# Six additions of output weights, moved from VectorE to a copy and an accumulating DMA

## The chip, the core and the metric

The kernel runs on one core of a Trainium2 chip. The metric is the device time in microseconds of one execution. The engines are named as the profile names them: PE is TensorE (matmuls), DVE is VectorE, ACT is ScalarE, POOL is GpSimd, and SP is the engine that issues most DMAs. Each engine works through its own instructions in order; a wait for a semaphore holds what stands behind it.

## The reference

Three steps follow each other on 4608 rows (tokens) of 512 columns: attention in chunks of 64, a gated layer with a norm, and a layer with a rational function.

```python
x = attention(q, k, v)                        # 8 x 8 heads, 576 rows, chunks of 64
xn = x / rms(x) * rms_g
g, val = xn @ w_gate, xn @ w_val              # 512 -> 1536
x = (g * sigmoid(g) * val) @ w_out            # 1536 -> 512
h = x @ w_in                                  # 512 -> 2048
P = a[0] + a[1] * h + a[2] * h**2 + a[3] * h**3
Q = 1 + abs(b[0]) * abs(h) + abs(b[1]) * h**2
out = (P / (Q + 1e-06)) @ w_out2              # 2048 -> 512
```

All is float32. The factors of `q` and `k` only set the spread of the inputs.

## The kernel before

Each float32 operand of a matmul is held as two words, a high one (rounded by ACT) and a low one (the rest, from a subtraction on DVE), and a product is three matmuls: high by high, high by low, low by high. The 4608 rows are nine blocks of 512. Many products are done with seven block products in place of eight, on sums and differences of quarters of both operands.

The work is a long list of turns. `at_turn` (L470) puts a step on a turn, `spread` (L638) puts the steps of a generator on successive turns, and `do` (L473) runs what a turn holds. Tables of turn numbers at the head of the file set where side work goes.

The change lies where the gate products end and the products with `w_out` begin, some 640 us into the program. `items` (L810) lists the latter: six items of block 0, called item 0 to item 5 below (24 matmuls each, plain, into the banks `a0_0` to `a0_3`), then items of 12 matmuls for pairs of blocks: B11 and B21 on plain weights, T2, T1, T3 and B22 on sums of weights (`so`), N4 on plain ones. Item 0 is on turn 252, the first item with `so` (T2) on turn 264.

For each item `high` (L882) casts the high word on ACT and `low` (L886) subtracts for the low word on DVE (L891), three items ahead, into `rring`, which has four places; a place is free once PE has done with its item. `uring` holds what `fetch` loads from `ud`.

`left_sums` (L830) makes the sums of weights for `f` = 0, 2, 4. It adds the two words of a weight back together (L835, two additions of 128x1024 into the pair `xo`), forms four sums of quarters (L839, 128x512 each), and splits them into `so` (L846 on ACT, L848 on DVE). `xo` takes buffers of the tag "t", of which there are three; `stage_left` has them for its raw weights (`raw2`) before. `LEFT_SUMS_AT` (L46) is the table of its turns, four steps to a turn.

In this stage only ACT keeps the order in which the code is written:

```python
        with tc.manual_schedule(engines={mybir.EngineType.Activation}):
```

DVE, PE, SP and POOL are ordered by the scheduler of the library, from its own estimates, when the program is built. The last instructions of the stage before are those of `finish` (L549): L511 and L558 work on the last gate products (`sa`), and L558 frees their PSUM banks, which `a0_1` takes next.

Of the kernel before, what the change touches and what calls it, by code (L numbers as in the profile page):

```python
# [9 lines left out]
F32 = mybir.dt.float32  # L10
# [4 lines left out]
ALU = mybir.AluOpType  # L15
# [7 lines left out]
U = 4  # L23
# [19 lines left out]
OPEN_AT = 237  # L43
START_AT = (244, 252)
QUAD_AT = (277, 271, 270, 274, 288, 285, 289, 288, 299, 304, 294, 307, 305, 320, 324, 324)
LEFT_SUMS_AT = (255, 254, 264)  # L46
EARLY = 3
BLOCK0 = (
    (-20, "fetch", 0), (-18, "ring", 0), (-17, "split", 0, "B11"), (-16, "split", 0, "B21"), (-15, "sum", 0, "T1"),
    (-14, "split", 0, "T1"), (-14, "sum", 0, "T3"), (-12, "ring", 1), (-11, "split", 0, "B22"), (-10, "sum", 0, "T2"),  # L50
# [6 lines left out]
def fused_kernel(  # L57
# [11 lines left out]
    nc = tc.nc  # L69
# [74 lines left out]
    buffers = {}  # L144
# [28 lines left out]
    def stage(f):  # L173
        words = raw_tile(2 * f + 1)
        yield
        hi, lo = (s2([P, W], f"{n}q_{f}", F32R) for n in ("hi", "lo"))
        yield from words_to_pair(*words, lambda: (hi, lo))
        for n, x in enumerate((hi, lo)):
            nc.sync.dma_start(out=wqd[f // U][:, n, f % U], in_=x.bitcast(F32))
        yield  # L180
# [3 lines left out]
    def stage_left(g):  # L184
        one, two = (raw_tile(4 * g + 2 * n) for n in range(2))
        yield
        yield from words_to_whole(*one)
        yield from words_to_whole(*two)
        x, y = (w[0].bitcast(F32) for w in (one, two))

        def put(at, x, name):
            hi, lo = (s2([P, W], f"{n}{name}_{g}", F32R)[:, :x.shape[1]] for n in ("hi", "lo"))
            yield from split(x, hi, lo)
            for n, z in enumerate((hi, lo)):
                nc.sync.dma_start(
                    out=wld[g][:, at:at + x.shape[1] // (2 * P), n, :],
                    in_=z.bitcast(F32).rearrange("p (k c) -> p k c", c=2 * P),
                )
            yield

        yield from put(0, x, "a")
        yield from put(6, y[:, W // 2:], "d")
        a11, a12, a21, a22 = (z[:, k * W // 2:(k + 1) * W // 2] for z in (x, y) for k in range(2))
        for o, i, j, op in ((a22, a21, a22, ALU.add), (a21, a11, a21, ALU.subtract), (a11, a22, a11, ALU.subtract), (a12, a12, a11, ALU.subtract)):
            nc.vector.tensor_tensor(out=o, in0=i, in1=j, op=op)
            yield
        yield from put(2, x, "s")
        yield from put(4, y, "u")
# [261 lines left out]
    def at_turn(turn, what, *of):  # L470
        plan.setdefault(turn, []).append((what, of))
# [166 lines left out]
    def spread(turn, steps, gap=1, each=1, most=60):  # L638
        for n in range(most):
            for _ in range(each):  # L640
                at_turn(turn + n * gap, next, steps, None)
# [54 lines left out]
    with ExitStack() as phase:  # L696
# [13 lines left out]
        def two_halves(source, u, keys):  # L710
            one, other = (unit(source, u, keys, p) for p in halves)
            next(one)
            next(other)
            yield
            yield from one
            yield from other
# [57 lines left out]
        for g in range(NF2 // 2):  # L774
            steps = stage_left(g)
            at_turn(STAGE_AT[g], next, steps)
            spread(STAGE_FROM[g], steps, 1, STAGE_EACH[g], 24 // STAGE_EACH[g])
        for u in range(3):
            steps = two_halves("wo", u, outs[u])
# [23 lines left out]
        with tc.manual_schedule(engines={mybir.EngineType.Activation}):  # L803
            KH = NF1 // 2
# [25 lines left out]
            def left_sums(f):  # L830
                xs = [sb.tile([P, 2, W], F32, tag="t", bufs=3, name=f"xo{f}_{n}") for n in range(2)]
                for n, x in enumerate(xs):
                    u, k = divmod(f + KH * n, U)
                    w = buffers["wo", u][1][:, :, k:k + 2].bitcast(F32)
                    nc.vector.tensor_tensor(out=x, in0=w[:, 0], in1=w[:, 1], op=ALU.add)  # L835
                    yield
                (a11, a21), (a12, a22) = ((x[:, :, :W // 2], x[:, :, W // 2:]) for x in xs)
                for o, x, y, op in ((a22, a21, a22, ALU.add), (a21, a11, a21, ALU.subtract), (a11, a22, a11, ALU.subtract), (a12, a12, a11, ALU.subtract)):
                    nc.vector.tensor_tensor(out=o, in0=x, in1=y, op=op)  # L839
                    yield  # L840
                for n, x in enumerate(xs):
                    u, k = divmod(f + KH * n, U)
                    w = sums_o[u][:, :, k:k + 2]
                    for m in range(2):
                        wt["so", f + KH * n + m] = w[:, :, m]
                    nc.scalar.copy(w[:, 0], x)  # L846
                    yield
                    nc.vector.tensor_tensor(out=w[:, 1], in0=x, in1=w[:, 0].bitcast(F32), op=ALU.subtract)  # L848
                    yield
# [8 lines left out]
            for n in range(NF2):  # L858
                steps = stage(n)
                at_turn(QUAD_AT[n], next, steps)  # L860
                spread(QUAD_AT[n] + 3, steps, 1, 2, 5)
            for f in range(0, KH, 2):
                spread(LEFT_SUMS_AT[f // 2], left_sums(f), 1, 4, 3)

            def sums_of(i):
                if i >= len(items) or items[i][0] is None:
# [89 lines left out]
            for t in range(NSB):  # L956
                running = {}
                used = 0
                for q, k in ORDER:
# [5 lines left out]
                    while True:  # L965
                        u = used // 8 + 2
# [24 lines left out]

            for turn, what, *of in BLOCK0:
                at_turn(end_o + turn, {"fetch": fetch_x2, "ring": x2_ring, "split": x2_split, "sum": x2_sum, "lefts": load_lefts,
                                       "work": make_work, "gg": make_gg, "quad": make_quad}[what], *of)

            def prepare(i):
                do(TURN[0])
                high(i + LEAD)
                sums_of(i + LEAD + 1)
                low(i + LEAD)  # L1000
# [47 lines left out]
            whole_acc, banks = [], []  # L1048
            for i in range(len(items) - 2 * EARLY):
                prepare(i)  # L1050
# [4 lines left out]
    def last_items():  # L1055
        for i in range(len(items) - 2 * EARLY, len(items)):
            prepare(i)
            todo = list(item_products(i))
            for n, of in enumerate(todo):
                nc.tensor.matmul(**of)  # L1060
                if n + 1 == len(todo):
                    item_end(i)
                yield

    with tc.manual_schedule(engines={mybir.EngineType.Activation, mybir.EngineType.DVE, mybir.EngineType.PE}):
# [76 lines left out]
        for p in range(NPAIR + 3):  # L1142
# [28 lines left out]
            if c is not None:  # L1171
                Tc = T_of.pop(c).rearrange("p e w -> p (e w)")
                r = ring["gg"][:, c % 2]
                for e in range(2):
# [3 lines left out]
                        out=r[:, 1, es], in0=Tc[:, es], in1=r[:, 0, es].bitcast(F32), op=ALU.subtract  # L1178
# [97 lines left out]
```

## Time and profile before

| what | us |
|---|---|
| median of 3 runs | 1670.3 |
| the three runs | 1670.16 to 1670.75 |
| the profiled execution | 1669.83 |
| its span, first to last instruction | 1668.0 |
| PE busy | 1656.3 |
| DVE busy | 1436.5 |
| ACT busy | 1055.7 |
| POOL busy | 331.0 |

The span is the time between the first and the last instruction of the profiled execution; 1.83 us of that execution lie around it. PE is busy 99% of the span. The granted TensorE clock is a share of full speed, 2.4 GHz.

### The profile page before, as it was taken

How to read it: one execution, taken by the hardware profiler on the slowest of the kernel's cores; microseconds unless marked ns; L12 is line 12 of the kernel's file. 1: busy time of each engine (PE TensorE's matmuls, PEld its weight loads, DVE VectorE, ACT ScalarE, POOL GpSimd, SP SyncE). 2: the span in 40 equal slices, each digit the busy share in tenths (PEclk: the TensorE clock that was granted, in tenths of full speed). 3: DMA queues.
4: the chain of work that ended last, by engine and by line, in shares of the span. 5: the costliest groups of instructions: out<-in, count | busy, mean ns of one | idle time of the engine just before them, and what ended most of it. 6: DMA issues, size and time to landing. Idle time of an engine off the chain costs nothing.

```text
span 1668.0 us, 28366 instructions
## 1 busy us (share of the span) xinstructions
PE 1656.3 (99%) x10956; PEld 1424.0 (85%) x10956; DVE 1436.5 (86%) x1762; ACT 1055.7 (63%) x1592; POOL 331.0 (20%) x286
## 2 busy tenths in 40 slices
PE   9999999999999999999999999999999999999999
PEld 7788888888888887888888899898999999989897
DVE  7978878877788788898997899999999999999986
ACT  7734445555465563566566777777777777777775
POOL 1000000000000000000012334343343434343321
PEclk9999999999999999999999999999999999999999
DMA  9547997878988998468757865655555555555551
GB/s 336 216 161 241 338 316 268 321 254 322 339 293 308 378 340 291 151 228 284 249 170 290 325 209 195 202 202 201 198 195 198 195 199 197 202 198 202 177 196 63
DMA packets 138694, 402.41 MB, mean 241 GB/s; under 512 B 13504, under 2 KB 58560, under 8 KB 124736
## 3 DMA queue, kind: packets, MB, share of 16 engines
q1 hardware_dynamic: 138416, 400.35, 67.9%
q8 instruction: 86, 1.41, 0.3%
q10 hardware_dynamic: 144, 0.26, 0.1%
q14 instruction: 48, 0.39, 0.1%
HBM read 308.29 MB, written 92.27 MB: 240 GB/s over the span
## 4 chain that ended last, share of the span: by engine, by line
PE 96%; DVE 1%; ACT 1%; DMA 1%; issue 1%; POOL 0%; DVEq 0%
PE o L1100 24%; PE h L1081 22%; PE sa L538 11%; PE sb L538 9%; PE ob L1052 6%; PE oa L1052 6%; PE v L501 5%; PE g L501 5%; PE xs L290 2%; PE a L1052 2%; PE tp L357 1%; PE tp L360 1%; PE ob L1060 0%; PE oa L1060 0%; DMA raw<-in_w_dram 0%
## 5 line engine op out<-in xcount | busy, mean ns | idle before, releaser
L1100 PE MATMUL o<-w,ggring 128*128 128x512 f32 x1728 | 418.6, 391 | 0.0
L1081 PEld LDWEIGHTS h<-x2ring,lefts 128*128 128x128 f32 x2982 | 377.3, 191 | 13.9 <-PE h L1081 2.1
L1081 PE MATMUL h<-x2ring,lefts 128*128 128x256 f32 x2982 | 382.7, 283 | 1.0 <-ACT both L1188 0.2
L1100 PEld LDWEIGHTS o<-w,ggring 128*128 128x128 f32 x1728 | 315.2, 188 | 60.6 <-POOL ggring L1177 0.5
L1177 POOL TENSOR_TENSOR ggring<-T,ggring 128x512 fp32r<-128x512 f32 x142 | 181.6, 1299 | 406.1 <-ACT ggring L1176 406.1
L671 POOL TENSOR_TENSOR x2ring<-x2r,x2ring 128x512 fp32r<-128x512 f32 x63 | 116.6, 1857 | 450.4 <-PE oa L1052 356.9
L1156 ACT ACTIVATE work<-h 128x1024 f32<-128x1024 f32 x72 | 73.9, 1026 | 164.7 <-PE h L1081 163.7
L884 ACT CAST rring<-uring 128x1024 fp32r<-128x1024 f32 x90 | 94.0, 1051 | 76.4 <-PE oa L1052 24.5
L1193 DVE SCALAR_TENSOR_TENSOR work<-work 128x1024 f32<-128x1024 f32 x72 | 133.9, 1860 | 2.5
L891 DVE TENSOR_TENSOR rring<-uring,rring 128x1024 fp32r<-128x1024 f32 x90 | 112.2, 1255 | 18.4 <-ACT rring L884 18.2
L1158 DVE SCALAR_TENSOR_TENSOR work<-work,small 128x1024 f32<-128x1024 f32 x72 | 92.1, 1280 | 27.8 <-ACT work L1157 27.8
L538 PE MATMUL sa<-right,left 128*128 128x512 f32 x432 | 111.2, 394 | 0.0
L501 PE MATMUL g<-xT,w 128*128 128x512 f32 (+1 forms) x444 | 109.9, 391 | 1.3 <-ACT w L135 0.6
L538 PE MATMUL sb<-right,left 128*128 128x512 f32 x432 | 108.8, 392 | 0.0
L501 PE MATMUL v<-xT,w 128*128 128x512 f32 (+1 forms) x444 | 106.5, 387 | 0.0
L1194 DVE SCALAR_TENSOR_TENSOR T<-T,small,work 128x1024 f32<-128x1024 f32 x72 | 99.9, 1387 | 2.5
L339 POOL TENSOR_SCALAR ssq<-ssq 128x1 f32<-128x1 f32 x36 | 7.3, 204 | 452.1 <-ACT xf L337 438.0
L501 PEld LDWEIGHTS g<-xT,w 128*128 128x128 f32 x444 | 80.1, 188 | 18.1 <-DVE w L137 0.9
L538 PEld LDWEIGHTS sb<-right,left 128*128 128x128 f32 x432 | 80.3, 188 | 16.9 <-DVE u L511 0.3
L501 PEld LDWEIGHTS v<-xT,w 128*128 128x128 f32 x444 | 80.8, 188 | 16.2
L1161 DVE SCALAR_TENSOR_TENSOR T<-T,small,h 128x1024 f32<-128x1024 f32 x72 | 92.2, 1281 | 2.5
L538 PEld LDWEIGHTS sa<-right,left 128*128 128x128 f32 x432 | 79.9, 188 | 16.2
(190 smaller groups left out, 2972.5 us busy)
## 6 DMA issues: line engine op xcount, KB each, us to landing
lefts<-wld SPq DMA_DIRECT2D x71, 1536.0 KB, 6.5
left<-wsd SPq DMA_DIRECT2D x30, 2048.0 KB, 9.8
ud<-u SPq DMA_DIRECT2D x108, 256.0 KB, 3.4
uring<-ud SPq DMA_DIRECT2D x54, 512.0 KB, 5.8
raw<-in_w_dram SPq DMA_DIRECT2D x36, 512.0 KB, 6.2
lefts<-wld SPq DMA_DIRECT2D x71, 256.0 KB, 2.8
wsd<-cb SPq DMA_DIRECT2D x48, 256.0 KB, 3.6
raw<-in_w_dram SPq DMA_DIRECT2D x10, 1024.0 KB, 9.8
```

Of the source, the lines that this page charges most:

```text
L501: nc.tensor.matmul(out=acc[:, ts], lhsT=w[:, wh, wk], rhs=x[:, kk, xh, ts], start=kk == 0 and n == 0, stop=kk == KD - 1 and n == 2,)
L538: nc.tensor.matmul(out=acc, lhsT=lhs[:, wh, kk * P:(kk + 1) * P], rhs=rhs[:, kk, xh, :], start=start and kk == 0 and m == 0, stop=kk == 1 ...
L671: nc.gpsimd.tensor_tensor(out=lo, in0=x, in1=hi.bitcast(F32), op=ALU.subtract)
L884: nc.scalar.copy(slot(i)[0], u_of(*items[i]))
L891: nc.vector.tensor_tensor(out=lo, in0=u_of(t, n, f), in1=hi.bitcast(F32), op=ALU.subtract)
L1052: nc.tensor.matmul(**of)
L1081: nc.tensor.matmul(out=out_, lhsT=lhs[:, wh, kk * P:(kk + 1) * P], rhs=rhs[:, kk, xh, :], start=start and kk == 0 and m == 0, stop=kk == 1 ...
L1100: nc.tensor.matmul(out=acc2[j][m], lhsT=ring["gg"][:, p % 2, rh, e * W + m * P:e * W + (m + 1) * P], rhs=ring["quad", f // U][:, wh, f % U ...
L1161: nc.vector.scalar_tensor_tensor(out=T, in0=T, scalar=a1, in1=H, op0=ALU.add, op1=ALU.mult)
L1177: (nc.vector if c == NPAIR - 1 else nc.gpsimd).tensor_tensor(out=r[:, 1, es], in0=Tc[:, es], in1=r[:, 0, es].bitcast(F32), op=ALU.subtract)
L1193: nc.vector.scalar_tensor_tensor(out=V, in0=V, scalar=-2.0, in1=R, op0=ALU.add, op1=ALU.mult)
L1194: nc.vector.scalar_tensor_tensor(out=T, in0=T, scalar=a0, in1=V, op0=ALU.add, op1=ALU.mult)
```

## The change

In `left_sums` the two additions L835 are replaced by DMAs, in two steps: SP copies the high word of both weights into `xo`, and POOL then issues two DMAs that add the low word to what lies in `xo`. The first step is put on a turn of its own, `SUM_AHEAD` = 2 turns ahead of the rest. The table of turns changes from (255, 254, 264) to (256, 262, 253), so that `f` = 4 now comes first, then `f` = 0, then `f` = 2. In the changed program the lines behind L835 stand further down: L839 is L845, L846 is L852, L848 is L854, L891 is L899.

```diff
--- before.py
+++ after.py
@@ -43,8 +43,9 @@
 OPEN_AT = 237
 START_AT = (244, 252)
 QUAD_AT = (277, 271, 270, 274, 288, 285, 289, 288, 299, 304, 294, 307, 305, 320, 324, 324)
-LEFT_SUMS_AT = (255, 254, 264)
+LEFT_SUMS_AT = (256, 262, 253)
 EARLY = 3
+SUM_AHEAD = 2
 BLOCK0 = (
     (-20, "fetch", 0), (-18, "ring", 0), (-17, "split", 0, "B11"), (-16, "split", 0, "B21"), (-15, "sum", 0, "T1"),
     (-14, "split", 0, "T1"), (-14, "sum", 0, "T3"), (-12, "ring", 1), (-11, "split", 0, "B22"), (-10, "sum", 0, "T2"),
@@ -832,8 +833,13 @@
                 for n, x in enumerate(xs):
                     u, k = divmod(f + KH * n, U)
                     w = buffers["wo", u][1][:, :, k:k + 2].bitcast(F32)
-                    nc.vector.tensor_tensor(out=x, in0=w[:, 0], in1=w[:, 1], op=ALU.add)
-                    yield
+                    nc.sync.dma_start(out=x, in_=w[:, 0])
+                yield
+                for n, x in enumerate(xs):
+                    u, k = divmod(f + KH * n, U)
+                    w = buffers["wo", u][1][:, :, k:k + 2].bitcast(F32)
+                    nc.gpsimd.dma_start(out=x, in_=w[:, 1], accum_op=ALU.add)
+                yield
                 (a11, a21), (a12, a22) = ((x[:, :, :W // 2], x[:, :, W // 2:]) for x in xs)
                 for o, x, y, op in ((a22, a21, a22, ALU.add), (a21, a11, a21, ALU.subtract), (a11, a22, a11, ALU.subtract), (a12, a12, a11, ALU.subtract)):
                     nc.vector.tensor_tensor(out=o, in0=x, in1=y, op=op)
@@ -860,7 +866,9 @@
                 at_turn(QUAD_AT[n], next, steps)
                 spread(QUAD_AT[n] + 3, steps, 1, 2, 5)
             for f in range(0, KH, 2):
-                spread(LEFT_SUMS_AT[f // 2], left_sums(f), 1, 4, 3)
+                steps = left_sums(f)
+                at_turn(LEFT_SUMS_AT[f // 2] - SUM_AHEAD, next, steps)
+                spread(LEFT_SUMS_AT[f // 2], steps, 1, 4, 3)
 
             def sums_of(i):
                 if i >= len(items) or items[i][0] is None:
```

The one-line label that came with the change names something else (the last output tile's products in runs of 256 columns, each half stored by itself). The diff has nothing of that; this text goes by the diff.

How the instructions move, at three places. A name such as `xo4_1` is buffer 1 of the pair for `f` = 4. DMAHW and DMASW are the semaphores of DMAs that were issued by SP and by POOL.

On DVE, at the end of the gate products and the start of block 0, before:

```order
L558 TENSOR_TENSOR u7_9_6727<-u7_9_6727,sa2_9_6741 128x512 [waits PE_49]
L511 SCALAR_TENSOR_TENSOR u7_11_6951<-u7_11_6951,sa2_10_6767 128x512 [waits DMAHW7_49,Activation_49]
L835 TENSOR_TENSOR xo2_1_7045<-w2_6709 128x1024
L558 TENSOR_TENSOR u7_11_6951<-u7_11_6951,sa2_11_6789 128x512 [waits DVE_49,PE_49]
L839 TENSOR_TENSOR xo2_1_7045<-xo2_0_7044,xo2_1_7045 128x2x256 [waits DVE_49]
L835 TENSOR_TENSOR xo0_0_7078<-w0_6352 128x1024
L891 TENSOR_TENSOR rring1_6738<-uring1_6736,rring1_6738 128x2x512 [waits DMAHW1_49,Activation_49]
L891 TENSOR_TENSOR rring0_6737<-uring1_6736,rring0_6737 128x2x512 [waits DMAHW3_49,Activation_49]
L891 TENSOR_TENSOR rring1_6738<-uring1_6736,rring1_6738 128x2x512 [waits DMAHW2_49,Activation_49]
L839 TENSOR_TENSOR xo2_0_7044<-xo2_0_7044 128x2x256 [waits DVE_49]
L839 TENSOR_TENSOR xo2_0_7044<-xo2_1_7045,xo2_0_7044 128x2x256 [waits DVE_49]
L839 TENSOR_TENSOR xo2_1_7045<-xo2_1_7045,xo2_0_7044 128x2x256 [waits DVE_49]
```

and now:

```order
L559 TENSOR_TENSOR u7_9_6727<-u7_9_6727,sa2_9_6741 128x512 [waits PE_49]
L512 SCALAR_TENSOR_TENSOR u7_11_6951<-u7_11_6951,sa2_10_6767 128x512 [waits DMAHW7_49,Activation_49]
L559 TENSOR_TENSOR u7_11_6951<-u7_11_6951,sa2_11_6789 128x512 [waits DVE_49,PE_49]
L845 TENSOR_TENSOR xo4_1_6955<-xo4_0_6954,xo4_1_6955 128x2x256 [waits DMASW1_49,DMASW0_49]
L845 TENSOR_TENSOR xo4_0_6954<-xo4_0_6954 128x2x256 [waits DVE_49]
L845 TENSOR_TENSOR xo4_0_6954<-xo4_1_6955,xo4_0_6954 128x2x256 [waits DVE_49]
L845 TENSOR_TENSOR xo4_1_6955<-xo4_1_6955,xo4_0_6954 128x2x256 [waits DVE_49]
L899 TENSOR_TENSOR rring1_6738<-uring1_6736,rring1_6738 128x2x512 [waits DMAHW2_49,Activation_49]
L899 TENSOR_TENSOR rring0_6737<-uring1_6736,rring0_6737 128x2x512 [waits DMAHW3_49,Activation_49]
L899 TENSOR_TENSOR rring1_6738<-uring1_6736,rring1_6738 128x2x512 [waits DMAHW7_49,Activation_49]
L899 TENSOR_TENSOR rring0_6737<-uring1_6736,rring0_6737 128x2x512 [waits DMAHW0_49,Activation_49]
```

Before, L835 stood ahead of the last L558 and between the others; the low words of items 2, 1 and 3 (the three L891) came ahead of the last three L839. Now the last L558 follows L511 directly, and the four L845 of `f` = 4, which wait for both accumulating DMAs, stand ahead of all the low words (L899: items 2, 1, 3 and 4).

On SP, some 15 us ahead of that place, before:

```order
L824 DMA uring1_6736<-ud_0_74 128x1024 [waits DMAHW1_49]
L824 DMA uring1_6736<-ud_0_74 128x1024 [waits DMAHW2_49]
L828 DMA uring0_6735<-ud_2_76 128x1024 [waits DMAHW3_49,DVE_49]
L514 DMA ud_8_82<-u8_8_6652 128x512 [waits DMAHW4_49,DVE_49]
L195 DMA wld_7_94<-his_7_6888 128x2x256 [waits DMAHW5_49,Activation_49]
L195 DMA wld_7_94<-los_7_6889 128x2x256 [waits DMAHW6_49,DVE_49]
L514 DMA ud_8_82<-u8_10_6885 128x512 [waits DMAHW7_49,DVE_49]
L824 DMA uring1_6736<-ud_0_74 128x1024 [waits DMAHW0_49]
```

and now:

```order
L836 DMA xo4_0_6954<-w1_6514 128x1024 [waits DMAHW1_49]
L825 DMA uring1_6736<-ud_0_74 128x1024 [waits DMAHW2_49]
L829 DMA uring0_6735<-ud_2_76 128x1024 [waits DMAHW3_49,DVE_49]
L515 DMA ud_8_82<-u8_8_6652 128x512 [waits DMAHW4_49,DVE_49]
L196 DMA wld_7_94<-his_7_6888 128x2x256 [waits DMAHW5_49,Activation_49]
L196 DMA wld_7_94<-los_7_6889 128x2x256 [waits DMAHW6_49,DVE_49]
L515 DMA ud_8_82<-u8_10_6885 128x512 [waits DMAHW7_49,DVE_49]
L836 DMA xo4_1_6955<-w2_6709 128x1024 [waits DMAHW0_49]
```

The copies into `xo4_0` and `xo4_1` stand in places that loads into `uring1` had (items 3 and 4 of block 0); these loads now come after the last store to `ud`.

On PE, in item 1 of block 0, before:

```order
L1052 MATMUL a0_0_6989<-rring0_6737,w0_6352 128x512 [waits Activation_49]
L1052 MATMUL a0_0_6989<-rring0_6737,w0_6352 128x512 [waits DVE_49]
L1052 MATMUL a0_0_6989<-rring0_6737,w0_6352 128x512
L1052 MATMUL a0_1_6990<-rring0_6737,w0_6352 128x512 x3
```

and now:

```order
L1060 MATMUL a0_0_6993<-rring0_6737,w0_6352 128x512 [waits Activation_49]
L1060 MATMUL a0_1_6994<-rring0_6737,w0_6352 128x512
L1060 MATMUL a0_2_6995<-rring0_6737,w0_6352 128x512
L1060 MATMUL a0_3_6996<-rring0_6737,w0_6352 128x512
L1060 MATMUL a0_0_6993<-rring0_6737,w0_6352 128x512 [waits DVE_49]
L1060 MATMUL a0_0_6993<-rring0_6737,w0_6352 128x512
```

The scheduler has pulled the products of item 1 that need only the high word, one for each bank, ahead of the first that waits for DVE's low word.

## Rows read from the trace of the kernel before

**Rows 1.** The page, part 1: busy us (share of the span) and instructions.

```profile
PE 1656.3 (99%) x10956; PEld 1424.0 (85%) x10956; DVE 1436.5 (86%) x1762; ACT 1055.7 (63%) x1592; POOL 331.0 (20%) x286
```

**Rows 2.** Busy time by stretch, 620 to 700 us; the columns stand first.

```profile
core 0: us, PE busy (x) PEld busy (x) DVE busy (x) ACT busy (x) POOL busy (x), PEclk, DMA share, GB/s
...
620.00:640.00 20.00, 20.00 (x89) 16.30 (x87) 16.90 (x29) 10.20 (x17) 0.00 (x0) 1.00 0.96 304
640.00:660.00 20.00, 18.72 (x83) 15.47 (x83) 16.46 (x19) 6.81 (x8) 0.00 (x0) 1.00 0.98 368
660.00:680.00 20.00, 20.00 (x90) 16.56 (x89) 20.00 (x20) 8.08 (x9) 0.00 (x0) 1.00 0.24 79
680.00:700.00 20.00, 20.00 (x90) 16.55 (x89) 19.67 (x21) 11.51 (x14) 0.00 (x0) 1.00 0.30 93
```

**Rows 3.** Waits of PE, 580 to 720 us: total us, times, longest.

```profile
PE a L1052 <- DVE u L558: 1.3, 1, 1.3
```

**Rows 4.** Timeline of DVE: start us, us, instruction, count [idle before <-what ended it].

```profile
628.55 0.69 DVE L570 TENSOR_TENSOR c<-c,sb 128x512 f32<-128x512 f32 x1 [2.90 <-PE sb L538]
...
638.89 0.68 DVE L511 SCALAR_TENSOR_TENSOR u<-u,sa 128x512 f32<-128x512 f32 x1
639.49 1.21 DVE L835 TENSOR_TENSOR xo<-w 128x1024 f32<-128x1024 f32 x1
640.62 0.68 DVE L558 TENSOR_TENSOR u<-u,sa 128x512 f32<-128x512 f32 x1
...
642.96 3.48 DVE L891 TENSOR_TENSOR rring<-uring,rring 128x1024 fp32r<-128x1024 f32 x3
646.37 0.68 DVE L839 TENSOR_TENSOR xo<-xo 128x512 f32<-128x512 f32 x1
647.08 1.42 DVE L839 TENSOR_TENSOR xo<-xo,xo 128x512 f32<-128x512 f32 x2
```

**Rows 5.** Timeline of PE, the same columns.

```profile
639.23 0.84 PE L1052 MATMUL a<-rring,w 128*128 128x512 f32 x3
641.36 32.25 PE L1052 MATMUL a<-rring,w 128*128 128x512 f32 x141 [1.28 <-DVE u L558]
673.45 8.32 PE L1052 MATMUL oa<-rring,w 128*128 128x512 f32 x36
681.61 8.32 PE L1052 MATMUL ob<-rring,w 128*128 128x512 f32 x36
689.77 8.32 PE L1052 MATMUL oa<-rring,so 128*128 128x512 f32 x36
```

**Rows 6.** Timeline of SP, 634 to 635 us.

```profile
634.58 0.51 SPq L824 DMA_DIRECT2D uring<-ud  x1
```

**Rows 7.** DMA issues of 634.5 to 635.0: count, KB each, median us to landing.

```profile
uring<-ud SPq DMA_DIRECT2D x1, 512.0 KB, 5.8
```

**Rows 8.** All loads into uring from 600 to 720 us.

```profile
DMA to landing us min/median/max: 3.6/5.9/10.4
```

**Rows 9.** DMA issues of 642.1 to 642.6 us.

```profile
uring<-ud SPq DMA_DIRECT2D x2, 512.0 KB, 6.4
```

**Rows 10.** Busy time by stretch at the end (columns of rows 2).

```profile
1664.00:1666.00 2.00, 0.25 (x2) 0.00 (x0) 0.00 (x0) 0.60 (x1) 0.00 (x0) 1.00 0.47 181
1666.00:1668.00 2.00, 0.00 (x0) 0.00 (x0) 0.00 (x0) 0.00 (x0) 0.00 (x0) 0.78 0.21 81
```

**Rows 11.** Busy time of POOL alone: us, busy (count), clock, DMA share, GB/s.

```profile
560.00:820.00 260.00, 0.00 (x0) 1.00 0.75 261
```

**Rows 12.** The page, part 6: DMA issues of the whole program.

```profile
raw<-in_w_dram SPq DMA_DIRECT2D x10, 1024.0 KB, 9.8
```

**Rows 13.** DMA issues of 590 to 710 us.

```profile
raw<-in_wo_dram SPq DMA_DIRECT2D x2, 1024.0 KB, 14.7
```

## The prediction

> **What bounds the kernel now.** I read the page first: PE is busy 1656.3 us of a span of 1668.0, DVE 1436.5 [rows 1]. Nothing else comes near, so time can only be won where PE waits, and lost where PE is made to wait. A gain of all PE's idle time would be 11.7 us, start and end of the program included. Then the stretches around the changed lines: from 620 to 700 us PE is busy in full but for 1.28 us in 640 to 660, while DVE is busy 16.46 to 20.00 us of each 20, and the DMA engines are nearly full (0.96, 0.98) until 660 and nearly idle behind it [rows 2]. Then PE's own waits from 580 to 720: there is one, 1.3 us, and it ends with DVE's L558 [rows 3]. The two timelines tell why: the last L558 frees the PSUM bank that the block-0 product needs; it runs at 640.62 because an L835 addition of 1.21 us stands ahead of it at 639.49 [rows 4], and PE, which had done three matmuls at 639.23, goes on at 641.36 [rows 5].
>
> Against the median of 1670.3 the profiled execution (1669.83, span 1668.00) is 0.47 us short. About 0.2%, 3.3 us, is what a measurement of this kernel can tell from no change.
>
> **The change, part by part.**
>
> The additions taken off DVE: six L835 of 1.2 us, 7.3 us of DVE work. PE waited for DVE only once here [rows 3], so only the one at 639.49 is on PE's path. Without it the last L558 can start at 639.49, where that addition started, instead of 640.62: gain 640.62 - 639.49 = 1.13 us, and PE goes on at 641.36 - 1.13 = 640.23. The addition at 600 gives nothing: DVE idles 2.90 us, waiting for PE, before 628.55 [rows 4]. The other four stand where PE never waits.
>
> The wait that comes in. The order of the changed program has the four L845 (the old L839) of f = 4 right behind the last L558 on DVE, and the first of them waits for both accumulating DMAs of f = 4. DVE works in order, so the low word of block-0 item 1 (second L899) waits with them. PE needs that low word 25 matmuls after 640.23: 21 left of item 0 and the four products of item 1 that need only the high word. A matmul takes 8.16 us / 36 = 0.227 us (from the 36 at 673.45 to the next at 681.61 [rows 5]), so PE gets there at 640.23 + 25 x 0.227 = 645.9.
>
> When the data are there. The later of the two copies, xo4_1, takes the place on SP of the fetch that is issued at 634.58 [rows 6]; it can't go sooner, as its buffer is read by the low-word split of `stage_left` until just before. That fetch has the same 512 KB and lands 5.8 us later [rows 7], so the copy lands at 640.4. Shortest and longest for 512 KB in 600 to 720 us are 3.6 and 10.4 [rows 8]. The trace of before has no accumulating DMA and no DMA from POOL here. I bound it by the same two, 3.6 and 10.4, and take 6.4: the two fetches issued around 642.1 to 642.6, when the backlog of uring loads that the accumulation will meet begins [rows 9]. A gain isn't excluded below: a fast copy and a fast accumulation would leave only the 1.13. Landing: 640.4 + 6.4 = 646.8.
>
> DVE behind it: four L845 (three took 646.37 to 648.50, so four take 2.8 us) and two L899 (three took 3.48, two take 2.35) [rows 4], 5.1 us together: item 1's low word is there at 651.9. PE's wait: 651.9 - 645.9 = 6.0 us. It has nothing else to do meanwhile, and as PE bounds all that follows, the 6.0 are not caught up.
>
> The clock. After PE's last matmul the granted clock is 1.00 to 1666 and 0.78 in the last 2 us [rows 10]: part of that stretch is at 1.2 GHz, with PE idle. So a wait of several us may be followed by matmuls at 1.2 GHz, which no row here shows. Nothing below; above, as long as the wait itself at half speed, 3 us lost. I take 1 us. The Trainium skill (TensorE: Matmul & The Clock Gate, Part 1) says that the low clock is the default and that activity releases it; the end of the trace agrees as to the fall, and no row shows the rise.
>
> What costs nothing. The six copies and six accumulations (6.3 MB written) use DMA engines that are at 0.24 and 0.30 from 660 to 700 [rows 2]; only those of f = 4 fall into the full stretch, and that is in the landing times above. POOL has no other work from 560 to 820 us [rows 11]. SP issues six DMAs more, some 0.4 us each; the fetches of items 3 and 4 slip behind the last `ud` store (from 625 and 634 to about 641), but PE comes to item 3 only 16 us after 640. The new table gives f = 4 and f = 0 first and f = 2 last, its copies two turns ahead; the first matmul on `so` is at 689.77 [rows 5]. For f = 0 the copies are issued behind item 4's low word, which needs PE's end of item 0, and the DVE row that waits for their accumulations stands behind item 7's, which needs the end of item 3: 3 x 24 x 0.227 = 16.3 us of matmuls cover them. If that cover is gone, the same kind of wait comes again (rival three). Behind these, the `raw2` and `uring` loads of the next stage now wait for buffers of `xo`, but are used some 30 us later.
>
> Sum: 1669.83 - 1.13 + 6.0 + 1.0 = 1675.7; with the 0.47 to the median, 1676.2.
>
> **The rivals.**
>
> One: a longer accumulation, because the DMA engines read both the buffer and the addend, 1 MB for 512 KB. The nearest row is a 1024 KB load, 9.8 us [rows 12]. Landing 650.2, low word 655.3, wait 9.4: 1669.83 - 1.13 + 9.4 + 1.0 + 0.47 = 1679.6. For it: the backlog. Against: the accumulation is alone on POOL's queue, where the loads of [rows 9] stand in a line. 0.18. The Trainium skill (Collectives: The Full Stack, Part 3) states that an add inside the DMA needs two source reads and so twice the read traffic for each byte delivered; by that the sum is this rival's, and no run so far shows it.
>
> Two, on the other side: the accumulation lands in time. The place is the first L845; it decides at 645.9 - 5.1 = 640.8 for no wait at all, and at 640.8 + 1.1 + 3.3 = 645.2 for staying within 0.2%. A copy of 3.6 and an accumulation of 3.6 would land at 641.8: wait 1.0, time 1669.83 - 1.13 + 1.0 + 0.47 = 1670.2. For it: copy and accumulation stay inside SBUF, while the rows are loads from DRAM; against: DMA is at 0.98 there [rows 2]. 0.22.
>
> Three: accumulations are so slow that the second pair is late too. With 14.7 us (1024 KB loads in this stretch [rows 13]) the first wait is 14.3; the next pair, one behind the other, is then some 5 us late at its L845: 1669.83 - 1.13 + 14.3 + 2 + 5 + 0.47 = about 1690. 0.08.
>
> Faster by over 0.2% would need 3.3 us, and PE has 1.28 to give here [rows 2]: 0.02. The one-line label that came with the change speaks of the last output tile, of runs of 256 columns and of half stores; the diff has none of that, so no term for the end of the program is in the sum.
>
> **How the numbers follow.** Forecast 0.50; rivals 0.18, 0.22 and 0.08; a gain 0.02. Slower: 0.50 + 0.18 + 0.08 = 0.76; same 0.22; faster 0.02. The range goes from rival two's 1670.2, say 1670.0, to an accumulation of 10.4 with 3 us of clock: 1669.83 - 1.13 + 10.0 + 3 + 0.47 = 1682.2, say 1683.0. Rival three and a gain, 0.10, are outside, with some of the cases between.
>
> **What would show it.** In the changed kernel PE's wait before a_1 (1.28) shrinks to about 0.15, and a new one of some 6 us stands four matmuls into item 1, at about 646, released by DVE's L899; DVE is idle some 6 us before the first L845, released by a DMA; the later accumulation of f = 4 lands near 647. The granted clock of the stretch behind it tells whether the 1 us is right. I am wrong if PE has no wait above 1 us there, if the second L845 group is the one that stalls, or if PE loses time outside 636 to 700.

## The result, and the profile after

The changed kernel takes 1681.96 us (median of 4 runs, 1681.58 to 1684.11); the kernel before, on the same chip, 1670.53. The ratio is 1.007, 95% interval 1.0058 to 1.0082: slower by 11.4 us. The forecast was 1676.2, range 1670.0 to 1683.0, with 0.76 on slower. The profiled execution took 1682.25, its span 1680.5 against 1668.0.

PE's waits from 580 to 720 us, which answer to [rows 3]:

```profile
engine line waited for: us in total, times, longest us
PE a L1060 <- DVE rring L899: 8.8, 1, 8.8
PE a L1060 <- DVE u L559: 0.3, 1, 0.3
```

The wait before bank `a` shrank from 1.3 to 0.3, and a new one of 8.8 stands behind it, released by the low word. The timeline of PE, against [rows 5]:

```profile
636.34 4.24 PE L539 MATMUL sa<-rightn,left 128*128 128x512 f32 x18
640.42 0.84 PE L1060 MATMUL a<-rring,w 128*128 128x512 f32 x3
641.61 5.96 PE L1060 MATMUL a<-rring,w 128*128 128x512 f32 x25 [0.35 <-DVE u L559]
656.38 29.45 PE L1060 MATMUL a<-rring,w 128*128 128x512 f32 x116 [8.81 <-DVE rring L899]
685.66 8.32 PE L1060 MATMUL oa<-rring,w 128*128 128x512 f32 x36
```

It is at the forecast place: 25 matmuls, 21 of item 0 and four of item 1, then the wait. What DVE did meanwhile, against [rows 4]:

```profile
640.87 0.69 DVE L559 TENSOR_TENSOR u<-u,sa 128x512 f32<-128x512 f32 x1
651.18 0.69 DVE L845 TENSOR_TENSOR xo<-xo,xo 128x512 f32<-128x512 f32 x1 [9.63 <-DMA xo<-w]
651.91 0.69 DVE L845 TENSOR_TENSOR xo<-xo 128x512 f32<-128x512 f32 x1
652.63 1.42 DVE L845 TENSOR_TENSOR xo<-xo,xo 128x512 f32<-128x512 f32 x2
653.97 4.62 DVE L899 TENSOR_TENSOR rring<-uring,rring 128x1024 fp32r<-128x1024 f32 x4
```

DVE stood 9.63 us with nothing to do, until the second accumulation of f = 4 landed, and four low words stood behind it. The DMAs issued from 641 to 644 us give that accumulation its time, count, KB and us to landing; POOL issued it at 643.09, so it landed at 651.1:

```profile
xo<-w POOLq DMA_DIRECT2D x1, 512.0 KB, 8.0
uring<-ud SPq DMA_DIRECT2D x1, 512.0 KB, 7.6
```

Behind the wait the granted clock was low. Busy time by stretch, the columns of [rows 2]:

```profile
645.00:650.00 5.00, 2.57 (x12) 1.80 (x10) 0.00 (x0) 0.00 (x0) 0.00 (x0) 1.00 1.05 221
650.00:655.00 5.00, 0.00 (x0) 0.00 (x0) 3.71 (x5) 3.12 (x4) 0.00 (x0) 0.72 1.02 415
655.00:660.00 5.00, 3.62 (x9) 2.85 (x10) 5.00 (x6) 0.86 (x1) 0.00 (x0) 0.50 1.03 414
660.00:665.00 5.00, 5.00 (x18) 4.01 (x17) 0.87 (x1) 0.92 (x1) 0.00 (x0) 0.75 1.02 406
665.00:670.00 5.00, 5.00 (x23) 4.13 (x22) 1.22 (x1) 0.59 (x2) 0.88 (x1) 1.00 1.02 395
```

0.50 is 1.2 GHz. The 116 matmuls behind the wait took 685.66 - 656.38 = 29.3 us, at 0.227 each they would have taken 26.3: 3.0 us lost.

The sum over the profiled execution: 8.8 (new wait) + 3.0 (clock) - 0.9 (first wait) + 1.2 = 12.1 of the 12.4 us between 1682.25 and 1669.83. The 1.2 us lie ahead of the change: the 18 products into `sa` that end that stage start at 636.34 instead of 635.15. In the executions of the experiments below they start between 634.4 and 637.8, whatever the kernel, so I count it to the execution, not to the change. The medians bear that out: they lie 11.4 us apart, 1.0 less than these two executions.

### The profile page after: what moved, and what is told of

The parts are those of the page before. It is cut to its first block, busy times and chain, and to the rows that moved or that the text cites. A ratio compares the mean times of both kernels' runs of the same rounds, so it can differ in the third digit from the quotient of the medians.

```text
span 1680.5 us, 28400 instructions
## 1 busy us (share of the span) xinstructions
PE 1660.2 (99%) x10956; PEld 1426.8 (85%) x10956; DVE 1431.6 (85%) x1756; ACT 1056.4 (63%) x1592; POOL 337.0 (20%) x292
## 3 DMA queue, kind: packets, MB, share of 16 engines
q0 software_dynamic: 864, 3.15, 1.0%
## 4 chain that ended last, share of the span: by engine, by line
PE 95%; DVE 1%; ACT 1%; DMA 1%; issue 1%; POOL 0%; SPq 0%; POOLq 0%; DVEq 0%; ACTq 0%
PE o L1108 23%; PE h L1089 22%; PE sa L539 11%; PE sb L539 9%; PE ob L1060 6%; PE oa L1060 6%; PE g L502 5%; PE v L502 5%; PE xs L291 2%; PE a L1060 2%; PE tp L358 1%; PE tp L361 1%; DMA raw<-in_w_dram 0%; PE ob L1068 0%; PE oa L1068 0%
## 5 line engine op out<-in xcount | busy, mean ns | idle before, releaser
L899 DVE TENSOR_TENSOR rring<-uring,rring 128x1024 fp32r<-128x1024 f32 x90 | 112.2, 1257 | 24.7 <-ACT rring L892 24.3
```

What stands on the lines that cost most here:

```text
L899: nc.vector.tensor_tensor(out=lo, in0=u_of(t, n, f), in1=hi.bitcast(F32), op=ALU.subtract)
```

## Experiments

Each ran beside the kernel before, whose medians were 1670.5 to 1671.1; times are medians, profile lines are from one execution of each. Line numbers differ by some lines from kernel to kernel. Diffs are against the changed kernel where nothing else is said, and cut where they show `...`.

**Pair f = 4 by VectorE again.**

```diff
+                    if f == 4:
+                        nc.vector.tensor_tensor(out=x, in0=w[:, 0], in1=w[:, 1], op=ALU.add)
+                        yield
+                        continue
                     nc.sync.dma_start(out=x, in_=w[:, 0])
...
```

> The changed kernel with one part undone: the pair f=4 is added by two VectorE adds again, the pairs f=0 and f=2 stay copies plus accumulating DMAs, and the new table stays. Theory of the wait (all that was lost is the 8.8 us in which TensorE stood in item 1 behind pair f=4, and about 3.0 us at the lower clock after it): no wait in item 1, the granted clock 1.00 through 640 to 690 us, time 1670.5, within 1 us of the kernel before. Rival, load (the extra transfers slow the DMA queues and with them the stage): four of six pairs of transfers stay, so about 1678. Rival, table (the new order of the three pairs costs it): 1682.

1676.83 us, ratio 1.0035 [1.0023, 1.0048]: neither theory. The wait in item 1 is gone, as the first says, but another has come. PE's waits, and ScalarE's timeline ahead of the new one:

```profile
PE oa L1069 <- ACT x L922: 3.6, 1, 3.6
PE a L1069 <- DVE u L559: 1.3, 1, 1.3
```

```profile
674.80 1.99 ACT L860 CAST so<-xo 128x1024 fp32r<-128x1024 f32 x2 [9.87 <-DVE xo L853]
676.70 1.04 ACT L901 CAST rring<-uring 128x1024 fp32r<-128x1024 f32 x1
677.64 1.07 ACT L922 ACTIVATE x<-a 128x512 f32<-128x512 f32 x2
```

The second pair, f = 0, is late as well. ScalarE works in order too: its casts of that pair wait 9.87 us, and behind them stands the eviction of bank `a`, which PE needs empty before `oa`. In the changed kernel the same wait does not show: PE comes there 11.0 us later (685.66 against 674.67), the pair's last accumulation lands only 6.7 us later (679.2 against 672.5). The profiled execution took 1674.54, 2.3 us less than the median.

**The table alone** (against the kernel before).

```diff
-LEFT_SUMS_AT = (255, 254, 264)
+LEFT_SUMS_AT = (256, 262, 253)
```

> The kernel before with the changed table 256, 262, 253 alone; all six adds stay on VectorE. Theory of the wait: 1670.5, within 1 us of the kernel before, since the one VectorE add ahead of the last L558 is still there and nothing waits for a DMA. Rival, table: part or all of 11.4 us, up to 1682.

1670.42 us, 0.9998 [0.9989, 1.0007]. The table costs nothing by itself.

**Pair f = 4 alone by DMA.**

```diff
+                    if f != 4:
+                        nc.vector.tensor_tensor(out=x, in0=w[:, 0], in1=w[:, 1], op=ALU.add)
+                        yield
+                        continue
                     nc.sync.dma_start(out=x, in_=w[:, 0])
...
```

> The complement of the first experiment: pair f=4 by copies and accumulating DMAs, pairs f=0 and f=2 by VectorE adds again. Theory of masking (each pair that comes by DMA would stall TensorE at its own place, but the 11.8 us that pair f=4 costs move TensorE back so far that the pairs behind it arrive in time): pair f=4 alone costs what all three cost together, a wait of 8 to 9.5 us in item 1 with the first wait back at 0.3 to 1.3 us, so 1681 to 1683. Rival, additive (each pair bears its own part of the 11.4 us; the first experiment lost 5.7 with the other two): 1676 to 1677.

1682.31 us, 1.0066 [1.0053, 1.0079]. PE's waits:

```profile
PE a L1069 <- DVE rring L908: 9.5, 1, 9.5
PE a L1069 <- DVE u L559: 1.3, 1, 1.3
```

Masking holds: f = 4 alone costs what all three cost (1682.0), the other two alone 5.7, and together they cost no more than the first. Additive fails by 5 us.

**All six by DMA, started behind the low words.**

```diff
-LEFT_SUMS_AT = (256, 262, 253)
+LEFT_SUMS_AT = ((254, 256, 257, 8), (258, 259, 260, 8), (261, 262, 263, 8))
...
+                copy, add, sums, each = LEFT_SUMS_AT[f // 2]
+                at_turn(copy, next, steps)
+                at_turn(add, next, steps)
+                spread(sums, steps, 1, each, 8)
```

> The changed kernel with all six copies and all six accumulating DMAs kept, but the three pairs started at turns 254, 258 and 261 in the order 0, 2, 4, which puts the first L845 behind seven low words on VectorE instead of ahead of them. Theory of the wait: TensorE's wait in item 1 goes, and the first wait stays at 0.2 to 0.4 us instead of 1.28, so 1669.5 to 1670; should the last pair land too late for the ninth item of the second kind, that shows as a wait on so at the place of T2 and adds its own length. Rival, load: the same six pairs of transfers cost the same, 1682.

1687.88 us, 1.0103 [1.0089, 1.0117]: a miss, the wrong way. The wait in item 1 is gone and the first wait is 0.3, but the later pairs stop PE at three other places:

```profile
PE oa L1062 <- ACT rring L894: 7.2, 1, 7.2
PE oa L1062 <- ACT x L915: 4.9, 1, 4.9
PE ob L1062 <- DVE rring L901: 0.9, 1, 0.9
```

None of them is the wait on `so` that I had allowed for; casts and evictions stand behind the sums on ScalarE and DVE. The number is above the rival's too. The four waits come to 13.2 us (one of 0.2 is not shown), and around the ends of the two long ones the granted clock is at 0.50, 1.2 GHz, from 676 to 682 and from 708 to 716 us: 36 products took 10.3 us there instead of 8.2, and 48 took 13.7 instead of 10.9.

**Filler on TensorE, first try.**

```diff
+FILL = 64
...
+                    if i == 1 and n == 4:
+                        idle = two_banks([P, P], "fill")
+                        for _ in range(FILL):
+                            nc.tensor.matmul(out=idle, lhsT=ident, rhs=ident, start=True, stop=True)
...
```

> The changed kernel with 64 products of the identity with itself (128x128, 0.128 us each by the row of the first stage, 8.2 us together) put on TensorE in item 1, ten ahead of the place where it waits and 54 at it. They are work that nobody reads. The wait on VectorE of 8.8 us stays, but TensorE is busy in most of it. If about 3.0 us are lost to the granted clock after the wait because TensorE stood still: clock 1.00 from 650 to 670, 116 matmuls after the wait in 26.3 instead of 29.3 us, time 1679.0. If the lower clock has another cause (the DMA traffic, the restart of the stage): 1682, and the clock of 655 to 665 is again 0.5 to 0.75.

1694.1 us, 1.0137 [1.0123, 1.0151]: inconclusive, my mistake. Each of these float32 products ran as two passes, and 108 of the 128 stood behind the wait:

```profile
656.89 1.22 PE L1065 MATMUL a<-rring,w 128*128 128x512 f32 x2 [6.84 <-DVE rring L900]
657.91 13.95 PE L1064 MATMUL fill<-ident 128*128 128x128 f32 x108
```

**Filler, second try.**

```diff
+FILL = 32
...
+                if i == 1:
+                    idle = two_banks([P, P], "fill")
+                    for _ in range(FILL):
+                        nc.tensor.matmul(out=idle, lhsT=ident, rhs=ident, start=True, stop=True)
                 for of in item_products(i):
```

> The filler of the run before put where it was meant to be: 32 fp32 products of the identity with itself, which run as 64 passes of 0.128 us, 8.2 us in all, on TensorE between item 0 and item 1. In the run before most of them stood behind the wait and lengthened it. If standing still is what lowers the granted clock: clock 1.00 from 650 to 670, the 116 matmuls behind the wait in 26.3 instead of 29.3 us, time 1678.5 to 1680. If the low clock has another cause: 1682 to 1683, and the windows from 655 to 665 are again at 0.5 to 0.75.

PE's timeline, and behind it busy time by stretch (PE alone, then clock, DMA share, GB/s):

```profile
647.95 7.30 PE L1063 MATMUL fill<-ident 128*128 128x128 f32 x64
655.01 0.47 PE L1065 MATMUL a<-rring,w 128*128 128x512 f32 x1
658.36 27.27 PE L1065 MATMUL a<-rring,w 128*128 128x512 f32 x119 [2.87 <-DVE rring L900]
688.15 8.45 PE L1065 MATMUL oa<-rring,w 128*128 128x512 f32 x36 [2.53 <-ACT x L914]
```

```profile
650.00:655.00 5.00, 5.00 (x48) 1.00 1.02 347
655.00:660.00 5.00, 2.13 (x11) 1.00 1.03 417
660.00:665.00 5.00, 5.00 (x24) 1.00 1.02 406
```

The clock stays at 1.00, and 119 matmuls take 27.27 us, within 0.3 of 0.227 each, with the DMA engines as full as before (1.02 to 1.03): the low clock came from PE standing still. But the kernel takes 1686.02 us (1.0094 [1.0081, 1.0108]), where I had expected 1678.5 to 1680. The profiled execution, at 1688.95 the longest of the four, shows where a part of that goes. Its stage had started 1.4 us later than in the changed kernel's, so what the clock gave back had brought PE to the end of `a` no earlier (685.6 in both). The second pair landed 2.1 us later (681.4 against 679.2), and PE met it: 2.53 us before `oa`, 1.8 us in `ob`, 0.6 at the products with `so`. These are 4.9 of the 6.7 us between the two profiled executions; the rest I did not trace. So the clock does give the 3.0 us back, but not to the kernel's time, because the second pair is behind.

**A plain copy in place of the accumulation.**

```diff
-                    nc.gpsimd.dma_start(out=x, in_=w[:, 1], accum_op=ALU.add)
+                    nc.gpsimd.dma_start(out=x, in_=w[:, 1])
```

> The changed kernel with the second DMA of each tile as a plain copy on the same queue, of the same 512 KB; it leaves out the addition of the low word to the high word in these sums. If the accumulation, which must read both operands, sets the 8.0 us (and the 4.5 to 7.0 of the later ones): the second DMA lands in about half of them, the wait in item 1 falls from 8.8 to 4 to 6, time 1677 to 1679. If the traffic that the queues carry at that point sets it: 7 to 8 us again, time 1681 to 1682.

1677.0 us, 1.0041 [1.0028, 1.0055], as the first theory has it. It leaves out the addition of the low word. PE's wait, and the DMA issued by POOL between 641 and 644:

```profile
PE a L1060 <- DVE rring L899: 4.8, 1, 4.8
```

```profile
xo<-w POOLq DMA_DIRECT2D x1, 512.0 KB, 5.5
```

The landing is 5.5 us instead of 8.0, not half. The shorter landing accounts for 2.5 of the 4.0 us by which the data are there sooner; the other 1.5 come from the copy of `xo4_1`, which took 4.6 us instead of 6.0 beside a plain DMA of the first tile. What doubles is the DMA engines' own time: the queue of POOL, from 616 to 700 us, packets, MB and share of 16 engines, in the changed kernel and in this one:

```profile
q0 software_dynamic: 864, 3.15, 20.4%
```

```profile
q0 software_dynamic: 864, 3.15, 9.6%
```

2.1 times for the same 3.15 MB. By the rule of the Trainium skill that the prediction cited (Collectives: The Full Stack, Part 3, where it is stated for the add of a collective: it needs two source reads) this is what one would see; the trace agrees in engine time, while the landing grew only about 1.5 times.

**The late copy from ScalarE's queue.**

```diff
-LEFT_SUMS_AT = (256, 262, 253)
+LEFT_SUMS_AT = ((254, 256, 256, 4), (260, 262, 262, 4), (246, 251, 253, 4))
...
-                    nc.sync.dma_start(out=x, in_=w[:, 0])
+                    (nc.scalar if f == 4 and n else nc.sync).dma_start(out=x, in_=w[:, 0])
...
```

The table now gives the turns of copy, accumulation and sums one by one; for f = 4 the copies are five turns and the accumulations two turns earlier in the code.

> The changed kernel with the copy of xo4_1 alone issued from ScalarE's queue, where it stands behind one cast that ends at 634.0, instead of from SP at 636.5; copies, accumulations and VectorE's order are otherwise the same. Theory of the wait (VectorE's idle time ends when the second accumulation lands): the copy and with it the landing come 1.5 to 2.5 us earlier and the wait in item 1 falls from 8.8 to 6.3 to 7.3 us. Theory of masking on top: what is gained there comes back in part at the place of the second pair, so the time lies between 1679 and 1682. Rival, one bound by the DMA engines (a transfer that starts earlier into full queues lands no earlier): the wait stays at 8.5 us or more.

1682.79 us, 1.0074 [1.0062, 1.0087]. The copy goes at 634.22 instead of 636.52, and the data are there at 650.4 instead of 651.1, although this execution's stage also ran 0.6 us earlier. PE's waits:

```profile
PE a L1062 <- DVE rring L901: 8.6, 1, 8.6
PE oa L1062 <- ACT x L915: 1.1, 1, 1.1
```

The rival is right: with the DMA engines at 1.0 and above, 2.3 us earlier at the issue is worth 0.1 to 0.2 at the landing. The copy took 6.8 us (6.0 before), the accumulation 8.6 (8.0). The wait of 1.1 us before `oa` is the second pair's again.

**Casts of f = 0 behind the evictions** (against the first experiment).

```diff
+                if f == 0:
+                    at_turn(LEFT_SUMS_AT[f // 2], next, steps)
-                spread(LEFT_SUMS_AT[f // 2], steps, 1, 4, 3)
+                spread(LEFT_SUMS_AT[f // 2] + 2 * (f == 0), steps, 1, 4, 3)
```

> The first experiment (pair f=4 on VectorE) with the sums and casts of pair f=0 two turns later, which puts ScalarE's two casts into so behind the evictions of bank a instead of ahead of them. If the 5.7 us of the first experiment were only the eviction L922 queued behind casts that waited for a DMA: the wait of 3.6 us before oa is gone, 1670.5 to 1672. If the pairs are bound as a chain (three buffers, a copy of about 10 us behind other loads, accumulations of 5 to 7 us one after the other): pair f=2 starts when pair f=0 lets its buffers go, is ready near 699 us and is wanted at 694, so about as much is lost at the first products that read its so, 1674 to 1677.

1675.03 us, 1.0028 [1.0018, 1.0039]. The number is the second theory's, the mechanism is not:

```profile
PE oa L1071 <- DVE x L922: 2.9, 1, 2.9
PE a L1071 <- DVE u L559: 1.3, 1, 1.3
```

There is no wait at the products that read `so`. ScalarE's eviction is in time now; the other half of bank `a` is evicted by DVE, where it stands behind the sums of the same pair. Behind the wait `ob` follows 9.04 us later, where 33 products of 0.227 take 7.5, so 2.9 + 1.5 = 4.4 us are explained of the 4.5 by which the median is longer. Pair f = 2 came in time after all: its last accumulation took 4.6 us, where 7.3 had been seen in the first experiment.

**Only f = 0 by DMA** (against the last).

```diff
-                    if f == 4:
+                    if f != 0:
                         nc.vector.tensor_tensor(out=x, in0=w[:, 0], in1=w[:, 1], op=ALU.add)
...
```

> As the last, with pair f=2 on VectorE too: only pair f=0 is copied and accumulated by DMA, wanted at 691 us and landing near 672.5. If what costs is a pair that is wanted before it lands, and nothing else of the DMAs: no wait at the products that read so, at most 1 to 2 us before oa where the VectorE evictions stand behind its sums, 1670.5 to 1672.5. If the traffic itself costs: more than 1673.

1674.47 us, 1.0019 [1.0010, 1.0029]: by the number the second theory's. But the wait is where the first one expected it, and the low clock takes as much again (`ob` follows at 686.18, 9.25 us later):

```profile
676.93 9.41 PE L1071 MATMUL oa<-rring,w 128*128 128x512 f32 x33 [1.78 <-DVE x L922]
```

1.8 + (9.25 - 7.5) = 3.5 of 4.0 us. That leaves little for traffic, which the next run tests.

**The same with all evictions of `a` on ScalarE, ahead of the casts** (against the last).

```diff
-                    if m % 2:
-                        nc.vector.tensor_scalar_mul(t, acc[m], 0.5)
-                    else:
-                        nc.scalar.mul(t, acc[m], 0.5)
+                    nc.scalar.mul(t, acc[m], 0.5)
```

> The run before (only pair f=0 by DMA, 4.0 us over the kernel before: a wait of 1.8 us before oa and 1.9 us lost behind it) with the two evictions of bank a that stood on VectorE put on ScalarE, ahead of its casts; VectorE still stands still until the second accumulation lands near 672.5. If the price is only what stands in order behind a waiting instruction: no wait before oa, time within 0.7 us of the kernel before, 1670 to 1671.2. If the DMAs cost something by themselves (traffic, POOL's issues, SP's queue), or VectorE's idle time of 4 us makes low words late: 1672.5 or more.

1672.03 us, 1.0009 [1.0000, 1.0018], between the two. DVE still stands 4.85 us for the accumulation, and PE runs through it:

```profile
642.58 32.25 PE L1068 MATMUL a<-rring,w 128*128 128x512 f32 x141 [1.28 <-DVE u L559]
674.67 8.32 PE L1068 MATMUL oa<-rring,w 128*128 128x512 f32 x36
```

The wait before `oa` is gone. What is left, 1.2 us, is there as two short waits on `so` at 694 us (0.24 and 1.05), where DVE is late with a later pair that it adds itself. So this pair by DMA costs PE nothing by its traffic that I could measure (the interval reaches to 3.0 us); it costs what stands behind it. For f = 4, whose transfers fall into the stretch with full DMA engines, I did not run the like.

**Adds on GpSimd, no DMA** (against the kernel before, with the new table).

```diff
-                    nc.vector.tensor_tensor(out=x, in0=w[:, 0], in1=w[:, 1], op=ALU.add)
+                    nc.gpsimd.tensor_tensor(out=x, in0=w[:, 0], in1=w[:, 1], op=ALU.add)
```

> No DMA: the kernel before with the changed table, and the six adds as GpSimd instructions, which is idle there for 133 us. A GpSimd add of 128x512 takes 1.3 to 1.9 us by the rows of the kernel before, so one of 128x1024 about 2.6 to 3.7, two for a pair 5 to 7.5, against about 17 to 21 us for a copy and an accumulation. If the chain length of a pair is what costs (the work itself may well leave VectorE): no wait in item 1, the first wait 0.3 to 1.0 instead of 1.28, 1669.5 to 1670.5, which is not to be told from the kernel before. If GpSimd's adds slow VectorE's beside them by more than a few tenths each, or pair f=4 is late again: above 1672.

1675.36 us, 1.0029 [1.0018, 1.0041]. The second alternative: PE waits 2.8 us for the last L558 and 1.8 before `oa`. The second add of f = 4 ran on POOL from 638.15 for 2.77 us, and beside it DVE's L839, otherwise 0.68, took:

```profile
639.80 1.67 DVE L839 TENSOR_TENSOR xo<-xo,xo 128x512 f32<-128x512 f32 x1
```

No version here beats the kernel before by more than a measurement can tell.

## Why the prediction was right, and where its terms were off

- **Place and mechanism: right.** The wait stands four matmuls into item 1, released by L899, with DVE idle before the first L845 and a DMA ending that. With f = 4 alone it is all there (1682.31); with f = 4 taken back it goes.
- **First wait: right.** -1.13 was forecast, -0.93 came.
- **The time: off by 5.8 us, from two terms that were too small.** The forecast for the profiled execution was 1675.7, and it took 1682.25: 2.8 us of the difference are the wait, 2.0 the clock, 0.2 the first wait, 1.2 the stretch ahead of the change, 0.3 open.
- **Landing: mis-sized, 646.8 against 651.1.** The copy was taken to land at 640.4 and landed at 642.5 (it took 6.0, not 5.8, but SP issued it 1.9 later, 1.2 of it the execution's own offset). POOL's issue 0.6 behind that was not in the sum. The accumulation, taken at 6.4 from plain loads, took 8.0. Rival one had the reason (two operands), and its 9.8 from a 1 MB load was too much; but its landing of 650.2 and its wait of 9.4 lie nearer to what came than the forecast's.
- **The wait: 6.0 forecast, 8.8.** Landing 4.3 later, DVE behind it 5.3 instead of 5.1, PE there 1.7 later: 6.0 + 4.3 + 0.2 - 1.7.
- **The clock: 1.0 taken, 3.0 came**, the upper bound I had kept. The filler shows that it is the standing still. The rule of the Trainium skill (TensorE: Matmul & The Clock Gate, Part 1), that activity is what releases the low clock, now has a row for the rise too: 0.50 at 655 to 660, 1.00 from 665 on.
- **"What costs nothing": right in the sum by luck, wrong in its reason.** I had written that 16.3 us of matmuls cover f = 0, and that the table costs nothing. The table doesn't. But the cover for f = 0 is not enough: without the wait in item 1, f = 0 and f = 2 cost 5.7 us, at a place where f = 0 is late, and f = 0 alone costs 4.0. I had looked only at low words and at `so` behind the waiting rows, not at the evictions of bank `a` behind ScalarE's casts and DVE's sums. The zero came out because the wait in item 1 moved PE back.
- **Rival two** (in time) fails by the landing, **rival three** (the second pair late too) is right that this pair has too little cover, but not in its reason (accumulations of 14.7 us; the longest in any run took 8.6) nor in the place, and the wait in item 1 hides it here.

Open: how much is lost at the low clock behind a wait of given length. 3.6 us before `oa` in the first experiment cost 0.1, 1.8 us in the run with f = 0 alone 1.8, 4.8 us with plain copies 1.6, 8.8 us 3.0, 9.5 us 2.1 (start to start, less 0.227 a matmul). These don't follow the length, and I tried nothing that tells what they do follow. Each is from one execution, and the same kernel need not repeat it: the first experiment's profiled execution, with 0.1 lost, took 1674.54 at a mean clock of 1.000, its other four 1676.08 to 1678.85 at 0.998 to 0.999. Not tried: more buffers for the pairs.

## What to carry to other kernels

Work that moves from an engine to DMAs leaves behind an instruction that waits for them, and on an engine that works in order the price is whatever stands behind that instruction, for every engine in the chain: here low words on DVE, then evictions on ScalarE, then evictions on DVE. An addition of 1.2 us was replaced by a chain of 14.6 us (the later one of f = 4, 636.5 to 651.1), and the two of f = 0 by one of 20 us (659.0 to 679.2), so ask first whether it was on the path at all. Late arrivals need not add up: here the first hid those behind it, so take them back one at a time, and don't read "no wait" behind a large wait as "in time".

## What the runs showed of the hardware that I had not expected

- Accumulating DMAs from POOL ran one after the other. POOL's timeline of the changed kernel:

```profile
668.78 0.88 POOL L841 DMA_DIRECT2D xo<-w  x1 [24.80 <-DMA xo<-w]
674.66 0.90 POOL L841 DMA_DIRECT2D xo<-w  x1 [4.99 <-DVE uring L884]
679.56 0.88 POOL L841 DMA_DIRECT2D xo<-w  x1 [4.01 <-DVE uring L884]
```

  The first took 5.6 us to land and the second 4.6: each next one was issued 0.3 us after the one before had landed, though its own copy was there sooner (669.5 for the second). Plain copies on the same queue were issued at 666.26 and 667.69 and took 5.3 and 5.1 us side by side. The built program is not what holds the next one back: in both kernels POOL's second DMA of f = 0 waits for its own copy, for DVE and for the first DMA of f = 4, not for the one just before it. An issue took POOL 0.88 to 1.05 us with accumulation and 0.54 to 0.76 without.
- SP's own issues took 1.02 to 1.36 us each from 635.4 to 641.6 us, where those of the same stretch took 0.32 to 0.62 before. What lengthens them I did not test.
- The granted clock can fall for a wait as short as 1.8 us, and then cost as much again (0.52 and 0.63 from 678 to 682 us with f = 0 alone by DMA). It need not: with the adds on GpSimd it stayed at 1.00 behind a wait of 1.76 us.
- A GpSimd add lengthened one of DVE's instructions beside it: the L839 above, both of whose operands lie in SBUF, from 0.68 to 1.67 us. The L558 and the L511 ahead of it, beside the same add, read one operand from a PSUM bank (`sa`) and took 0.68 each.
